# Zeros in place of the identity for TensorE's filling products, and transposes ahead of the modulation products, in an adaLN, sliding-window attention and gMLP kernel on one core

## The chip, the cores and the metric

One core of a Trainium2 chip runs the whole program in one launch. The metric is device time in microseconds (us), the median of several executions. Five engines work from queues of their own and meet at semaphores: TensorE (PE, matrix products; PEld is its weight load), VectorE (DVE), ScalarE (ACT), GpSimd (POOL) and SyncE (SP, which here issues nearly all DMAs).

## The reference, cut to what matters

One sequence of 2048 tokens, width D = 448, 16 heads of 28, window 256, and a gated MLP that mixes over tokens. Only the first stage bears on the change: the modulation rows, the first layer norm, and q, k, v of the first 512 tokens.

```python
mod = (_silu(c) @ w_mod).reshape(c.shape[0], 6, 1, -1)
sa, ca, ga, sb, cb, gb = (mod[:, i] for i in range(6))
h = _layernorm(x, axis=-1) * (1 + ca) + sa
x = x + ga * _A_ref(h, A_wqkv, A_wo)        # q, k, v; 16 heads; window 256; softmax
h = _layernorm(x, axis=-1) * (1 + cb) + sb
x = x + gb * _B_ref(h, B_w_in, B_w_sp, B_b_sp, B_w_out)   # gelu, layernorm, token mix
```

## The kernel before, in words

The 2048 tokens are 16 tiles of 128, in four blocks of 512. All operations are collected as numbered `Op`s with their dependences; the order in which each engine gets them is written out by hand in the table `ORDER` (line 19). A word such as `57.p.0` is operation 57 on PE with buffer 0 of its pool (p PE, a ACT, v DVE, g POOL, s SP). `Sched.order` (line 149) reads the table, and `Sched.waits` derives the semaphore waits. So an operation's number, given by the place in the code where it is added, and its place in the table are all that decides.

The head of the program works like this:

- SP issues loads: x in blocks of four tiles, `w_mod` in four chunks of rows for the first two modulation vectors (`t_wmA`) and the rest later (`t_wmB`, lines 407 and 408), the q, k weights in four chunks (`t_wq`), the v weights.
- DVE sets constants (lines 489 to 496), then computes the layer norm's statistics of tiles 0 to 3 (`stats`, lines 576 to 582, the power on POOL) and the normalised tiles `xn` (`norm`, line 589).
- PE turns the row c into a column (line 518). ACT makes silu of it, `sc_sb` (lines 522 and 523). Four groups of eight products with one column each (line 535), one for each chunk of `w_mod`, make the first two modulation vectors; DVE adds the four up into `modT` (line 540).
- PE transposes the four normalised tiles (line 620, eight at a time here), DVE and ACT scale and shift them with `modT` into `hT`, one chunk of 128 rows at a time (lines 630 and 631). The chunk `WQK` of the weights is copied into a padded layout by ACT, DVE and POOL (lines 568 and 569).
- 32 products of 512 columns (line 640), eight groups of four chunks, make q and k of the first 512 tokens in seven banks of PSUM; ACT and DVE take them out (lines 648 and 649). Then come first scores (line 849), values (line 660), the other modulation vectors as rows (line 553), and the transposes (line 708) of tiles 4 to 7, which POOL and DVE have normalised (lines 593, 595, 589); DVE's line 718 makes `hT` of them, and line 731 their q and k.

Between the real products PE runs filling products (`warm`, line 543): the identity times itself, into bank 5 of PSUM, which nothing reads. They depend on the identity (`t_ident`), which POOL makes at the start. 64 are declared, 40 with 512 columns and 24 with 128; those that the table names are issued, 13 of 512 and 12 of 128 columns.

Of the kernel before, what the change touches and what calls it, by code (L numbers as in the profile page):

```python
# [5 lines left out]
BF16 = mybir.dt.bfloat16  # L6
# [13 lines left out]
0.a 26.v 1.s 2.s 3.s 34.g 23.v 24.v 27.v 43.a 4.s 35.g 5.s 36.g 44.p.0 6.s 138.v 40.g 50.a 32.g 7.s 136.v 37.g 139.v 8.s 25.v 137.v 142.v 140.g 38.g  # L20
9.s 144.v 141.g 10.s 145.v 28.v 143.v 45.a 11.s 46.a 146.g 148.v.0 57.p.0 58.p.0 59.p.0 60.p.0 61.p.0 62.p.0 63.p.0 52.p.1 147.g 97.p.0 53.p 150.v.1
12.s 98.p.0 149.p.2.3 151.p 13.s 152.v.2 54.p 154.v.3 14.s 99.p.0 153.p 29.v 155.p 15.s 55.p 16.s 56.v 132.a 156.v 21.s 133.v 157.a 158.v 64.p.0
65.p.0 66.p.0 67.p.0 68.p.0 69.p.0 190.p.4 17.s 100.p.0 170.p.5 134.g 101.p.0 185.p.6 159.v 18.s 102.p.0 160.p.0 135.a 103.p.0 171.p 104.p.0 161.p
105.p.0 191.p 49.g 106.p.0 175.p.1 107.p.0 162.p 47.a 108.p.0 176.p 195.p.2 165.p.3 42.g 192.p 41.g 163.p 212.v 166.p 164.a 172.p 177.p 214.v 167.p
48.a 173.p 51.v 178.p 213.v 216.v 196.p 168.p 174.a 218.v 186.p 197.p 169.a 198.p 39.v 180.p.0 179.a 187.p 217.v 219.v 193.p 215.v 199.v 188.p 220.g
194.a 181.p 221.g 182.p 30.v 183.p 189.a 373.p.0 184.v 204.p.1 374.a.0 228.g 224.g 210.s 226.g 222.g 121.p.0 227.v.0 225.g.1 211.s 200.p.6 223.v.2
19.s 229.g.3 122.v 205.a 379.p.0 124.s 201.v 230.p.0 380.a.1 209.s 233.p.1 231.v 123.s 234.v 398.p.0 232.a 202.p.6 208.s 235.v 399.a.2 268.v 250.p.0
31.v 270.v 400.a 242.p.1 375.v 264.v 125.s 251.a 405.p.0 266.v 126.s 406.a.3 240.p.0 243.v 269.v 265.v 267.v 238.p.1 271.v 203.v 407.a 272.g 273.g
241.v 376.p.0 239.a 401.v 425.p.0 377.v 236.p.0 278.g 426.a.4.0 381.v 276.g 318.v 33.g 427.p.0 280.g 279.v.0 378.p 262.p.1 274.g 319.v 281.v.1 284.s
275.g.2 320.v 237.a 433.p.0 383.v 277.g.3 246.p.0 263.v 434.a.5.1 282.s 408.v 382.p 128.g 248.p.1 247.v 283.s 321.v 410.v 384.p 428.a 454.p.0 130.g  # L30
249.v 244.p.0 455.a.6.2 385.v 322.v 285.s 131.g 386.v.0 206.p.1 324.v 402.p.0 255.s 456.p.0 245.v 207.a 462.p.0 457.a 252.s 403.v 258.p.1 463.a.0.3
437.v 254.s 438.v 404.p 409.p 387.s 260.p.0 429.v 430.v 411.p 261.a 483.p.0 253.s 412.v 286.v 435.p.0 484.a.1.4 413.v.1 256.p.0 458.v 431.p.0 287.v
432.p 289.v 439.p 257.v 436.a 491.p.0 288.v 259.a 464.p.0 488.v 440.p 492.a.2.0 294.p.0 325.v 459.v 441.v 304.p.1 487.v 465.a 323.v 442.v.2 326.g
512.p.0 295.a 327.g 467.v 443.s 514.p.0 513.a.3.1 460.p.0 466.v 461.p 290.p.0 334.g 496.v 414.s 129.g 305.v 468.p 515.a 520.p.0 291.v 328.g 469.p
521.a.4.2 330.g 335.v.0 296.p.1 332.g 331.v.1 329.g.2 470.v 471.v.0 485.p.0 444.p.0 495.v 472.s 486.a 541.p.0 297.a 445.v 493.p.0 542.a.5.3 489.p.0
446.v 22.s 388.p.1 333.v.3 336.s 525.v 490.p 302.p.0 389.v 494.a 516.v 337.s 549.p.0 303.a 524.v 300.p.1 550.a.6.4 545.v 338.s 390.v 292.p.0 517.v
497.p 301.a 339.s 553.v 551.p.0 498.p 293.a 570.p.0 499.v 552.a 500.v.2 473.p.1 309.s 571.a.0.0 306.s 298.p.0 474.v 308.s 475.v 522.p.0 518.p.0 501.s
523.a 554.v 519.p 299.a 578.p.0 447.v 546.v 316.p.1 579.a.1.1 340.g 307.s 476.v 526.p 575.v 527.p 310.p.0 477.g 341.v 478.g 391.v 317.a 528.v 343.v
572.p.0 529.v.1 479.g 599.p.0 573.a 342.g 311.v 415.p.1 530.s 600.a.2.2 448.g 583.v 543.p.0 502.p.0 449.g 416.v 20.s 392.g 574.v 547.p.0 544.a 607.p.0
503.v 548.p 417.v 555.p 608.a.3.3 504.v 314.p.1 418.v 419.g 556.p 450.g 393.g 348.p.0 557.v 604.v 315.a 420.g 580.p.0 582.v 628.p.0 581.a 558.v.0  # L40
344.p.1 629.a.4.4 505.v 603.v 559.s 576.p.0 506.g 345.v 394.g 577.p 451.g.0 601.p.0 584.p 349.a 507.g 632.v 636.p.0 602.a 585.p 508.g 395.v.1
637.a.5.0 350.p.1 480.g.2 452.v 421.g 586.v 453.s 611.v 609.p.0 346.p.0 587.v.2 351.a 641.v 657.p.0 610.a 588.s 605.p.0 347.v 658.a.6.1 560.p.1 612.v
127.s 659.p.0 396.v 640.v 606.p 397.s 613.p 422.g.0 561.v 660.a 665.p.0 481.v 614.p 661.v 666.a.0.2 312.p.0 354.s 633.v 482.s 630.p.0 562.v 531.p.1
615.v 563.v 313.a 616.v.1 564.g 686.p.0 509.g.1 631.a 532.v 356.p.0 687.a.1.3 423.g 662.v 424.s 634.p.0 670.v 635.p 638.p.0 357.v 642.p 355.s 639.a
533.v 694.p.0 617.s 643.p 691.v 695.a.2.4 688.p.0 360.p.1 534.v 644.v 690.v 353.s 535.g 669.v 589.p.0 352.s 361.a 565.g 645.v.0 715.p.0 689.a 510.g
590.v 646.s 566.g 364.p.1 838.g 716.a.3.0 699.v 663.p.0 667.p.0 511.s 365.v 664.p 671.p 668.a 591.v 723.p.0 720.v 672.p 724.a.4.1 618.p.0 698.v 592.v
696.p.0 593.g 619.v 370.p.1 840.g 863.s 673.v 697.a 674.v.2 567.g.2 744.p.0 371.v 358.p.0 745.a.5.2 536.g 675.s 620.v 537.g 692.p.0 594.g 719.v 693.p
700.p 595.g 855.s 538.v.0 717.p.0 359.a 596.g.1 752.p.0 718.a 728.v 701.p 753.a.6.3 647.p.1 539.g 702.v 540.s 703.v.1 746.p.0 362.p.0 648.v 621.v
749.v 747.a 773.p.0 704.s 622.g 748.v 721.p.0 774.a.0.4 676.p.1 623.g 727.v 624.g 725.p.0 597.v 677.v 722.p 598.s 729.p 756.v 726.a 781.p.0 363.a
568.v 757.v 754.p.0 569.s 730.p 755.a 841.v 368.p.1 731.v 782.a.1.0 732.v.0 366.p.0 369.v 733.s 750.p.0 778.v 775.p.0 785.v 802.p.0 776.a 751.p 777.v  # L50
803.a.2.1 758.p 759.p 783.p.0 760.v 705.p.1 761.v.2 367.a 810.p.0 762.s 706.v 784.a 779.p.0 806.v 811.a.3.2 780.p 812.p.0 786.v 734.p.0 372.s 678.v
787.p 679.v 788.p 707.v 813.a 680.g 763.p.1 839.g 649.v 843.a 789.v 804.p.0 681.g 814.v 887.p.0 870.s 805.a 708.v 807.v 842.a 888.p.1 709.g 790.v.1
710.g 844.a 866.s 889.p 815.v 845.a 625.g.0 735.v 808.p.0 809.p 764.v 711.g 816.p 817.p 650.v 890.p 791.s 818.v 891.a 834.g 819.v.0 923.p.3 736.v
837.g 924.p.2 820.s 765.v 766.v 626.g 925.p 898.a 651.g 652.g 926.p 627.s 653.g 905.p.0 712.g.1 934.a 1031.p.1 682.g 713.v 893.v 767.g 927.a 836.g
714.s 906.p.2 654.v.2 907.p 655.v 935.v 656.s 792.p.0 683.v.0 909.a 684.g 832.g 821.p.1 793.v 685.s 900.v 908.p 768.g 822.v 941.p.0 769.g 916.a 910.v
# [211 lines left out]
def bass_adaLN_cond__sliding_block__mixer_gmlp__prompt_kernel(  # L267
# [42 lines left out]
    x_sb, _, _ = alloc("x_sb", [128, NT, D], BF16)  # L310
# [144 lines left out]
    def dve(dur, fn, deps=(), prio=0.0, take=()):  # L455
        return add({"dve": (dur, fn)}, deps, prio, take)
# [731 lines left out]
```

## Time and profile before

| | |
|---|---|
| median of three runs | 281.51 us (278.8, 281.51, 282.39) |
| the profiled execution | 280.97 us, span of its instructions 279.2 us |
| busy PE, DVE, ACT, POOL | 268.2, 164.0, 128.5, 110.6 us |
| filling products (line 546) up to 30 us | 25, 8.2 us busy |
| first q, k products (line 640) | 32, 7.6 us in all up to 19.4 us |

How to read it: the page's times are of one execution; its span runs from the first to the last instruction, and 1.8 us of the execution's time lie around it. The chain of waits is followed back from the last instruction to what released each step. The timeline lists instructions in order of time, with the start in us, the length of a row of equal instructions, the engine (SPq is SP's issue of a DMA), the line of the code, and in brackets the idle time ahead of it and what ended it. A matmul's length contains its way through the array, so back-to-back products are timed by their starts.

### The profile page before, as it was taken

Reading aid. Unit: us, or ns where it says so; the run is one execution under the profiler, and the core shown is the slowest. Engines: PE = TensorE matmul, PEld = TensorE weight load, DVE = VectorE, ACT = ScalarE, POOL = GpSimd, SP = SyncE. Lnnn points to the kernel's source line nnn. Section 1 sums busy time; section 2 is a strip of 40 time slices with the busy share of each in tenths; the row PEclk is TensorE's granted clock in tenths of the full one; section 3 lists DMA queues with packets and bytes.
Section 4 is the critical chain, followed back from the end, with each engine's and each line's share of the span. In section 5 each row is a group of like instructions: output and inputs, shape, how many; then the busy total and the mean of one; then the engine's idle time right before and its main releaser. Section 6 shows DMA issues by size and latency. Waiting matters only on the chain.

```text
span 279.2 us, 7360 instructions
## 1 busy us (share of the span) xinstructions
PE 268.2 (96%) x3204; PEld 140.8 (50%) x3204; DVE 164.0 (59%) x364; ACT 128.5 (46%) x152; POOL 110.6 (40%) x185
## 2 busy tenths in 40 slices
PE   5999999998999996999999999999999999999995
PEld 2644556565577574544444444444444444454452
DVE  7478999997899899578599501100240300242543
ACT  3579999997999997856767500000000000000000
POOL 4441824216634623676349401321271640271400
PEclk9999999999999999999999999999999999999999
DMA  6997472465744676949799999100000000001113
GB/s 191 302 263 159 103 88 32 90 85 137 158 69 70 95 105 70 215 76 187 86 166 207 170 181 196 20 0 0 0 4 0 0 0 2 0 0 33 57 63 112
DMA packets 66862, 26.48 MB, mean 95 GB/s; under 512 B 57801, under 2 KB 65742, under 8 KB 66830
## 3 DMA queue, kind: packets, MB, share of 16 engines
q1 hardware_dynamic: 66828, 26.01, 48.1%
q8 instruction: 25, 0.41, 0.7%
q14 instruction: 7, 0.06, 0.1%
q10 hardware_dynamic: 2, 0.00, 0.0%
HBM read 9.47 MB, written 1.84 MB: 41 GB/s over the span
## 4 chain that ended last, share of the span: by engine, by line
PE 80%; DVE 9%; POOL 4%; DMA 3%; ACT 2%; issue 1%
PE ps L1073 35%; PE ps L1090 7%; PE ps L1028 7%; PE ps L918 5%; PE ps L731 4%; PE ps L875 4%; PE ps L1049 4%; PE ps L943 3%; POOL rs_all L582 3%; DMA hT<-o_sb 3%; DVE st_all L576 3%; PE ps L773 2%; PE ps L640 2%; DVE PT L891 2%; PE ps L884 2%; PE ps L760 1%
## 5 line engine op out<-in xcount | busy, mean ns | idle before, releaser
L836 ACT ACTIVATE PW<-ps 128x2048 bf16<-128x2048 f32 (+1 forms) x56 | 67.2, 1243 | 7.2 <-PE ps L884 2.3
L1077 DVE TENSOR_TENSOR tmpg<-ps,bsp_bc 128x512 bf16<-128x512 f32 x28 | 19.0, 690 | 74.5 <-PE ps L1073 64.4
L1080 POOL TENSOR_TENSOR z1T<-tmpg,z1T 128x512 bf16<-128x512 bf16 x28 | 31.7, 1151 | 73.5 <-DVE tmpg L1077 73.5
L1073 PE MATMUL ps<-wspB,z 128*128 128x512 bf16 x224 | 49.5, 379 | 0.0
L1073 PE MATMUL ps<-wspA,z 128*128 128x512 bf16 x224 | 49.2, 379 | 0.1
L891 DVE TENSOR_TENSOR PT<-PW,mask 128x1024 bf16<-128x1024 bf16 x56 | 36.7, 681 | 0.3 <-ACT PW L836 0.3
L1073 PEld LDWEIGHTS ps<-wspA,z 128*128 128x128 bf16 x224 | 21.8, 98 | 26.8 <-DVE z L1040 0.6
L1073 PEld LDWEIGHTS ps<-wspB,z 128*128 128x128 bf16 x224 | 21.9, 98 | 26.3
L581 POOL TENSOR_SCALAR ve_all<-mv_all 128x1 f32<-128x1 f32 (+2 forms) x37 | 10.7, 296 | 48.2 <-DVE mv_all L579 47.6
L582 POOL TENSOR_TENSOR rs_all<-ve_all,neghalf 128x1 f32<-128x1 f32 (+2 forms) x37 | 25.5, 698 | 1.0
L918 PE MATMUL ps<-Vaug,PT 128*128 128x29 bf16 x496 | 24.9, 176 | 0.0
L918 PEld LDWEIGHTS ps<-Vaug,PT 128*128 128x128 bf16 x496 | 22.3, 96 | 4.4 <-DVE o_sb L934 1.0
L1028 PE MATMUL ps<-w_in,hT 64*128 64x448 bf16 x224 | 22.9, 349 | 0.0
L1049 PE MATMUL ps<-hT,w_in 64*128 64x512 bf16 x196 | 22.5, 376 | 0.0
L918 PE MATMUL ps<-Vaug,PW 128*128 128x29 bf16 x224 | 20.4, 175 | 0.6 <-issue 0.6
L1090 PE MATMUL ps<-w_out_g,z1T 128*128 128x448 bf16 x105 | 20.7, 352 | 0.0
L731 PE MATMUL ps<-hT,WQK 128*128 128x512 bf16 x80 | 20.1, 380 | 0.2 <-DVE qT L737 0.2
L576 DVE BATCH_NORM_STATS2 st_all<-x_sb 128x6 f32<-128x448 bf16 x32 | 19.0, 614 | 2.2 <-DMA x_sb<-in_A_x_dram 2.1
L576 DVE BATCH_NORM_STATS2 st_all<-z 128x6 f32<-128x448 bf16 x32 | 18.5, 605 | 2.1 <-ACT z L1035 1.9
L918 PEld LDWEIGHTS ps<-Vaug,PW 128*128 128x128 bf16 x224 | 17.7, 96 | 2.9 <-issue 0.7
L1057 ACT ACTIVATE z1T<-ps 128x512 bf16<-128x512 f32 x28 | 14.8, 610 | 7.1 <-PE ps L1049 7.0
L943 PE MATMUL ps<-wo_g,hT 128*128 128x448 bf16 x64 | 14.6, 353 | 3.4 <-DMA hT<-o_sb 3.4
(111 smaller groups left out, 330.8 us busy)
## 6 DMA issues: line engine op xcount, KB each, us to landing
out_dram<-fin SPq DMA_DIRECT2D x15, 112.0 KB, 1.7
x_sb<-in_A_x_dram SPq DMA_DIRECT2D x3, 448.0 KB, 6.8
w_in<-in_B_w_in_dram SPq DMA_DIRECT2D x1, 1344.0 KB, 7.4
wmod<-in_w_mod_dram SPq DMA_DIRECT2D x1, 1296.0 KB, 10.8
QBD<-qT SPq DMA_DIRECT2D x16, 64.0 KB, 3.0
w_out_g<-in_B_w_out_dram SPq DMA_DIRECT2D x1, 784.0 KB, 6.3
wmod<-in_w_mod_dram SPq DMA_DIRECT2D x3, 240.0 KB, 4.7
wq_st<-in_A_wqkv_dram SPq DMA_DIRECT2D x3, 224.0 KB, 5.5
```

Of the source, the lines that this page charges most:

```text
L576: st = [dve(0.62 if True else 0, lambda e, t=t, ci=ci, s=s: e.bn_stats(st_all[:, slot, t, ci, :], s()), deps(t), prio) for ci, s in enumer ...
L582: rs = pool(0.53 + 0.15 * len(tiles), lambda e: e.tensor_tensor(rs_all[:, slot, a:b], ve_all[:, slot, a:b], neghalf[:, 0:b - a], ALU.pow), ...
L731: m = pe(4 * MMS, [lambda e, h=h, g=g, kc=kc, tb=tb: e.matmul(ps[:, h.slot[0], :], lhsT=WQK[:, kc, 4 * g:4 * g + 4, :].rearrange("p a b -> ...
L836: ex = act(xdur, lambda e, out_ap=out_ap, in_ap=in_ap: e.activation(out_ap(), in_ap(), ACT.Exp, scale=SCALE), [s], v - 8.0 + u, takes, tab ...
L891: return dve(0.70, lambda e: e.tensor_tensor(cols(hp.slot[0] * 2048 + 1024 * k, [[256, 4], [128, 2], [1, 128]]), cols(at_w() + 128 + 192 * ...
L918: fns.append(lambda e, hp=hp, hO=hO, hi=hi, bi=bi, kb=kb, hd=hd, nb=nb, a=at[hi][bi], p_of=p_of: e.matmul(ps[:, hO.slot[0], 32 * hd:32 * h ...
L943: mo = pe(4 * MMD, [lambda e, h=h, j=j, ch=ch: e.matmul(ps[:, h.slot[0], 0:D], lhsT=hT[:, ch, j * 128:(j + 1) * 128], rhs=wo_g[:, ch, :], ...
L1028: return lambda e, kc, p0, start, stop: e.matmul(ps[:, hs[t % 2].slot[hf], 0:D], lhsT=hT[p0:p0 + 64, kc, t * 128:(t + 1) * 128], rhs=w_in[ ...
L1049: return lambda e, kc, p0, start, stop: e.matmul(ps[:, hs[b // 2].slot[b % 2], :], lhsT=w_in[p0:p0 + 64, kc, ft * 128:(ft + 1) * 128], rhs ...
L1073: m = pe(16 * MMS, [lambda e, h=h, si=si, ft=ft, tb=tb: e.matmul(ps[:, h.slot[0], :], lhsT=z2[:, si, ft * 128:(ft + 1) * 128], rhs=(wspA i ...
L1080: u = pool(1.16, lambda e, ht=ht, ft=ft, tb=tb: e.tensor_tensor(z1T[tb][:, ft, :], tmpg[:, ht.slot[0], :], z1T[tb][:, ft, :], ALU.mult), [ ...
L1090: return [lambda e, ft=ft: e.matmul(ps[:, h.slot[0], 0:D], lhsT=z1T[t // 4][:, ft, (t % 4) * 128:(t % 4 + 1) * 128], rhs=w_out_g[:, ft, :] ...
```

## The change

A tile `wz` of 128 x 128 bf16 is added and set to zero by DVE, as the first operation of the table. The filling products multiply `wz` by itself and wait for that memset instead of for the identity. 17 filling products are issued, all of 512 columns; the twelve of 128 columns are gone, nine of which stood among the q, k products. The new operation moves every later number up by one, so all words of the table read otherwise; the order on ACT, POOL and SP is the same, DVE's has the memset in front, and PE's differs up to the end of the q, k products.

```diff
+    wz, _, _ = alloc("wz", [128, 128], BF16)
...
+    t_wz = dve(0.08, lambda e: e.memset(wz[:], 0.0), prio=-99.9)
+
     def warm(n, dur, times, cols):
         for _ in range(n):
             hW = Hold(bH)
             hW.until.append(pe(dur, [lambda e, hW=hW: e.matmul(
-                ps[:, hW.slot[0], 0:128 * cols].rearrange("p (a b) -> p a b", b=128), lhsT=ident[:], rhs=ident[:].unsqueeze(1).broadcast_to([128, cols, 128]),
-                start=True, stop=True) for _ in range(times)], [t_ident], 900.0, [hW]))
+                ps[:, hW.slot[0], 0:128 * cols].rearrange("p (a b) -> p a b", b=128), lhsT=wz[:], rhs=wz[:].unsqueeze(1).broadcast_to([128, cols, 128]),
+                start=True, stop=True) for _ in range(times)], [t_wz], 900.0, [hW]))
```

The first words of the table, before and now:

```diff
-0.a 26.v 1.s 2.s 3.s 34.g 23.v 24.v 27.v 43.a 4.s 35.g 5.s 36.g 44.p.0 6.s
+57.v 0.a 26.v 1.s 2.s 3.s 34.g 23.v 24.v 27.v 43.a 4.s 35.g 5.s 36.g 58.p.0 59.p.0 60.p.0 44.p.0 6.s
```

PE's queue from its start to the end of the modulation, before. `ident` lines are fillers, `one,c_row` is the column of c, `sc_sb,wmod` the modulation groups, `ident,xn` the transposes:

```order
L518 MATMUL ps<-one,c_row 128x1 x3
L518 MATMUL ps<-one,c_row 64x1
L546 MATMUL ps<-ident 128x512 x7
L535 MATMUL ps<-sc_sb,wmod 128x1 x8
L546 MATMUL ps<-ident 128x128
L535 MATMUL ps<-sc_sb,wmod 128x1 x8
L546 MATMUL ps<-ident 128x128
L620 MATMUL ps<-ident,xn 128x128 x8
L535 MATMUL ps<-sc_sb,wmod 128x1 x8
L546 MATMUL ps<-ident 128x128
L620 MATMUL ps<-ident,xn 128x128 x8
L535 MATMUL ps<-sc_sb,wmod 128x1 x8
```

The same stretch now (line numbers are up by one to three; `wz` lines are fillers):

```order
L549 MATMUL ps<-wz 128x512 x3
L519 MATMUL ps<-one,c_row 128x1 x3
L519 MATMUL ps<-one,c_row 64x1
L549 MATMUL ps<-wz 128x512 x10
L623 MATMUL ps<-ident,xn 128x128 x8
L536 MATMUL ps<-sc_sb,wmod 128x1 x16
L549 MATMUL ps<-wz 128x512
L536 MATMUL ps<-sc_sb,wmod 128x1 x8
L623 MATMUL ps<-ident,xn 128x128 x8
L536 MATMUL ps<-sc_sb,wmod 128x1 x8
```

Three fillers stand ahead of the column of c and ten behind it, the first eight transposes come before the first two modulation groups, and one filler of 512 columns is left between the groups in place of three of 128.

PE's queue from the end of the modulation to the modulation rows (line 553), before; a product and a small filler alternate nine times:

```order
L546 MATMUL ps<-ident 128x512 x6
L640 MATMUL ps<-hT,WQK 128x512
L546 MATMUL ps<-ident 128x128
...
L640 MATMUL ps<-hT,WQK 128x512 x23
L849 MATMUL ps<-qT,KT 128x128 x8
L660 MATMUL ps<-wv,hT 128x448 x4
L553 MATMUL ps<-wmod,sc_rep 32x448 x16
```

and now:

```order
L549 MATMUL ps<-wz 128x512 x3
L643 MATMUL ps<-hT,WQK 128x512 x32
L852 MATMUL ps<-qT,KT 128x128 x8
L663 MATMUL ps<-wv,hT 128x448 x4
L556 MATMUL ps<-wmod,sc_rep 32x448 x16
```

Three fillers stand ahead of the q, k products in place of six, and none among them; what follows is unchanged.

More of the change, by code (lines that the diff above doesn't have):

```diff
@@ L24 @@
[L24 to L31, printed above, removed]
@@ L72 @@
[L72 to L74 removed]
+57.v 0.a 26.v 1.s 2.s 3.s 34.g 23.v 24.v 27.v 43.a 4.s 35.g 5.s 36.g 58.p.0 59.p.0 60.p.0 44.p.0 6.s 139.v 40.g 50.a 32.g 7.s 137.v 37.g 140.v 8.s
@@ new lines @@
+474.p.1 310.s 572.a.0.0 307.s 299.p.0 475.v 309.s 476.v 523.p.0 519.p.0 502.s 524.a 555.v 520.p 300.a 579.p.0 448.v 547.v 317.p.1 580.a.1.1 341.g
+308.s 477.v 527.p 576.v 528.p 311.p.0 478.g 342.v 479.g 392.v 318.a 529.v 344.v 573.p.0 530.v.1 480.g 600.p.0 574.a 343.g 312.v 416.p.1 531.s
+601.a.2.2 449.g 584.v 544.p.0 503.p.0 450.g 417.v 20.s 393.g 575.v 548.p.0 545.a 608.p.0 504.v 549.p 418.v 556.p 609.a.3.3 505.v 315.p.1 419.v 420.g
+557.p 451.g 394.g 349.p.0 558.v 605.v 316.a 421.g 581.p.0 583.v 629.p.0 582.a 559.v.0 345.p.1 630.a.4.4 506.v 604.v 560.s 577.p.0 507.g 346.v 395.g
@@ new lines @@
+578.p 452.g.0 602.p.0 585.p 350.a 508.g 633.v 637.p.0 603.a 586.p 509.g 396.v.1 638.a.5.0 351.p.1 481.g.2 453.v 422.g 587.v 454.s 612.v 610.p.0
+347.p.0 588.v.2 352.a 642.v 658.p.0 611.a 589.s 606.p.0 348.v 659.a.6.1 561.p.1 613.v 128.s 660.p.0 397.v 641.v 607.p 398.s 614.p 423.g.0 562.v 661.a
+666.p.0 482.v 615.p 662.v 667.a.0.2 313.p.0 355.s 634.v 483.s 631.p.0 563.v 532.p.1 616.v 564.v 314.a 617.v.1 565.g 687.p.0 510.g.1 632.a 533.v
+357.p.0 688.a.1.3 424.g 663.v 425.s 635.p.0 671.v 636.p 639.p.0 358.v 643.p 356.s 640.a 534.v 695.p.0 618.s 644.p 692.v 696.a.2.4 689.p.0 361.p.1
@@ new lines @@
+535.v 645.v 691.v 354.s 536.g 670.v 590.p.0 353.s 362.a 566.g 646.v.0 716.p.0 690.a 511.g 591.v 647.s 567.g 365.p.1 839.g 717.a.3.0 700.v 664.p.0
+668.p.0 512.s 366.v 665.p 672.p 669.a 592.v 724.p.0 721.v 673.p 725.a.4.1 619.p.0 699.v 593.v 697.p.0 594.g 620.v 371.p.1 841.g 864.s 674.v 698.a
+675.v.2 568.g.2 745.p.0 372.v 359.p.0 746.a.5.2 537.g 676.s 621.v 538.g 693.p.0 595.g 720.v 694.p 701.p 596.g 856.s 539.v.0 718.p.0 360.a 597.g.1
+753.p.0 719.a 729.v 702.p 754.a.6.3 648.p.1 540.g 703.v 541.s 704.v.1 747.p.0 363.p.0 649.v 622.v 750.v 748.a 774.p.0 705.s 623.g 749.v 722.p.0
@@ L75 @@
+1215.p.1 1188.v.3 1185.v.0 1216.p 1211.p.3 1186.s 1217.v.1 1218.s 1212.p 1189.s 1223.p.7 1213.v.2 1214.s 1220.p 1224.p 1178.p.6 1221.v.0 1225.v.1
+1222.s 1226.s 1179.v.3 1180.s
 """
```

87 lines of the change are left out of this document (40 added, 47 removed).

## The prediction, as put on record

> **What bounds the kernel now.** I read the page first, then the chain of waits in order of time over the first 35 us, then the timeline of that stretch engine by engine, then the DMA issues. The change touches only work before the first attention scores, so the question is what sets the end of that head, and who takes over from it.
>
> From the page, the span, the granted clock in 40 slices and the chain's shares by engine:
>
> ```profile
> span 279.2 us, 7360 instructions
> PEclk9999999999999999999999999999999999999999
> PE 80%; DVE 9%; POOL 4%; DMA 3%; ACT 2%; issue 1%
> ```
>
> The chain runs through PE for 80% of the span; whatever moves PE's queue as a whole is seen at the end. The chain's own rows in the head (start, length, engine, tile, line):
>
> ```profile
> 1.13 1.18 DVE wmod L491
> 9.81 2.16 PE ps L546 x6
> 14.41 4.96 PE ps L640 x23
> 20.46 0.87 PE ps L553 x16
> 21.33 0.86 PE ps L660 x4
> 22.20 0.22 PE ps L849 x8
> 22.42 0.57 PE ps L708 x8
> 23.01 1.00 DVE hT L718 x2
> ```
>
> So DVE's memsets and statistics open the chain, six filling products (L546) hold it for 2.16 us, the first q, k products (L640) until 19.4, then modulation rows and values, and at 22.4 the transposes (L708) of the next four tiles. What the fillers cost and at which speed TensorE ran is in its timeline:
>
> ```profile
> 2.60 0.35 PE L518 MATMUL ps<-one,c_row 1*128 1x1 bf16 x4 [2.60 <-DVE one L490]
> 2.89 3.17 PE L546 MATMUL ps<-ident 128*128 128x512 bf16 x7
> 7.38 1.06 PE L620 MATMUL ps<-ident,xn 128*128 128x128 bf16 x8
> 9.41 0.40 PE L535 MATMUL ps<-sc_sb,wmod 128*128 128x1 bf16 x8
> 9.67 2.30 PE L546 MATMUL ps<-ident 128*128 128x512 bf16 x6
> 11.80 0.38 PE L640 MATMUL ps<-hT,WQK 128*128 128x512 bf16 x1
> 12.08 0.38 PE L640 MATMUL ps<-hT,WQK 128*128 128x512 bf16 x1
> 14.25 5.13 PE L640 MATMUL ps<-hT,WQK 128*128 128x512 bf16 x23
> ```
>
> The seven fillers from 2.89 take 3.17 us; less the last one's latency that is 0.43 us for a 512-column product. The 23 products from 14.25 take 5.13 us, 0.216 us each. TensorE thus ran at half pace in the first stage although the page's row of granted clock prints a 9 everywhere. Five of the six fillers from 9.67 still ran at 0.43 (9.67 plus five times 0.426 is 11.80), so the pace doubled at about 11.4. Inside the q, k stage a product and the small filler behind it take 12.08 - 11.80 = 0.27 us, so a filler of 128 columns costs 0.055 us at full pace.
>
> By the Trainium skill, page TensorE: Matmul & The Clock Gate, section "What's actually happening", the clock gate opens after a sufficiently busy window of about 3.4 us of a free-running clock; the trace agrees that the pace is binary (0.43 against 0.216) and cannot show the window.
>
> **The change, part by part.** *The zeros.* A memset of 128 x 64 words is put first on DVE. Rows of memsets, two of which size it and the third of which is the last step before the modulation's input:
>
> ```profile
> 8.59 0.43 DVE L494 MEMSET wq_st<- 64x448 uint32 x1
> 18.70 0.24 DVE L495 MEMSET wv<- 64x224 uint32 x1
> 6.22 0.06 DVE L493 MEMSET sc_sb<- 1x1 bf16 x1
> ```
>
> Halving the columns takes off 0.19, which leaves 0.05 fixed and 0.06 for 64 columns: 0.11 us, and everything behind it on DVE starts that much later, since L491 and the statistics form the chain. PE pays 0.11 where it waits for the normalised tiles.
>
> *Fillers from 1.4 us.* The zeros are there at 1.24, so three fillers run from about 1.4 to 2.68 at 0.43. The products of c, queued behind them, start at 2.68 and not 2.60; nobody feels it, since DVE's own sc_sb step at 6.2 ends last for what follows. Then ten more: 4.3 us at the slow pace, to 7.25 at latest. The fillers cost nothing as long as they end before the normalised tiles come. Before, 3 us of fillers were followed by work of one column and transposes, and the pace doubled late. Now some 5.5 us of fillers stand almost without a gap. I take it that the pace doubles inside this run: 1.7 us of fillers sufficed from 9.67, with transposes ahead of them. The other bound is that it does not double until the q, k products, which is a rival below.
>
> *Transposes before the modulation.* The times of their inputs, and of what hangs on the modulation:
>
> ```profile
> 6.42 0.70 DVE L589 TENSOR_SCALAR xn<-x_sb,mv_all,rs_all 128x448 bf16<-128x448 bf16 x2
> 7.74 0.70 DVE L589 TENSOR_SCALAR xn<-x_sb,mv_all,rs_all 128x448 bf16<-128x448 bf16 x2 [0.61 <-POOL rs_all L582]
> 3.26 0.59 SPq L417 DMA_DIRECT2D wmod<-in_w_mod_dram  x1
> wmod<-in_w_mod_dram SPq DMA_DIRECT2D x1, 120.0 KB, 5.4
> 9.84 0.19 DVE L540 TENSOR_REDUCE modT<-ps 128x8 f32<-128x32 f32 x1 [0.82 <-PE ps L535]
> 10.07 0.54 DVE L631 TENSOR_SCALAR hT<-ps,modT 128x512 bf16<-128x512 bf16 x1
> 10.65 0.78 ACT L630 ACTIVATE hT<-ps,modT 128x512 bf16<-128x512 bf16 x1 [0.65 <-DVE hT L631]
> 10.99 0.93 POOL L569 COPY WQK<-wq_st 128x896 bf16<-128x896 bf16 x1 [3.29 <-DMA wq_st<-in_A_wqkv_dram]
> 11.53 0.95 ACT L568 ACTIVATE WQK<-wq_st 128x896 bf16<-128x896 bf16 x1
> ```
>
> Tile 1 is normalised at 7.12 + 0.11 = 7.23, so PE's transposes of tiles 0 and 1 end at about 7.5 (0.055 each at full pace, instead of 1.06 for eight, 0.85 of it without the tail). Two modulation groups of 0.26 (9.67 - 9.41) reach 8.0, a filler 8.2, the third group 8.5, the transposes of tiles 2 and 3 (input at 8.44 + 0.11) 8.95, the fourth group 9.2 and its result 9.35. Its weights were issued at 3.26 and need 5.4: they land at 8.66, in time. So modT's reduction starts at 9.35 in place of 9.84, and hT's first chunk (0.23 later, 0.54 long) is there at 10.12. The three fillers after the last group end at 9.85, ahead of it. q, k start at 10.15 and not 11.80: 1.65 us earlier. This term stands between -0.1 us (slow pace throughout: 7.25 + 0.85 + 0.52 + 0.43 + 0.26 + 0.85 + 0.4 = 10.56 for modT, three slow fillers from 10.4 to 11.7) and 1.65; I take 1.65, as the pace should have doubled.
>
> *No fillers inside q, k.* Nine of 0.055 go: 0.5 us. Their cover would be a wait for WQK. Its third chunk is ready at 10.99 + 0.93 = 11.92, set by a load; the ninth product needs it, and would be due at 10.15 + 8 x 0.216 = 11.88, so it waits under 0.1. The fourth chunk (11.53 + 0.95 = 12.48) is needed by the fourteenth product, due at 13.0: no wait.
>
> Sum to the end of q, k: 1.65 + 0.5 - 0.05 = 2.1 us earlier, 17.3 in place of 19.4.
>
> *What is late next.* The 2.1 us do not reach the next stage whole:
>
> ```profile
> 14.00 1.15 DVE L576 BATCH_NORM_STATS2 st_all<-x_sb 128x6 f32<-128x448 bf16 x2 [2.05 <-DMA x_sb<-in_A_x_dram]
> 17.71 0.23 POOL L581 TENSOR_SCALAR ve_all<-mv_all 128x4 f32<-128x4 f32 x1 [4.39 <-DVE mv_all L579]
> 19.18 0.96 POOL L593 TENSOR_SCALAR ve_all<-mv_all,rs_all 128x1 f32<-128x1 f32 x4
> 20.12 1.52 POOL L595 TENSOR_SCALAR xn<-x_sb,rs_all,ve_all 128x448 bf16<-128x448 bf16 x2
> 22.35 1.07 PE L708 MATMUL ps<-ident,xn 128*128 128x128 bf16 x16
> 7.78 0.51 SPq L407 DMA_DIRECT2D wmod<-in_w_mod_dram  x1
> 8.33 0.50 SPq L408 DMA_DIRECT2D wmod<-in_w_mod_dram  x1
> wmod<-in_w_mod_dram SPq DMA_DIRECT2D x1, 1296.0 KB, 10.8
> wmod<-in_w_mod_dram SPq DMA_DIRECT2D x1, 216.0 KB, 11.2
> ```
>
> Tiles 4 to 7 of x land at 14.00 and go through DVE's statistics, POOL's variance, scale and normalising without PE: the last two normalised tiles are ready at 20.12 + 1.52 = 21.64. L708 stood at 22.35 and can start no earlier than 21.68. The modulation rows (L553) wait for weights that land at 7.78 + 10.8 = 18.6 and 8.33 + 11.2 = 19.5, so PE, 2.1 us early, waits before them for about 1 us. From 19.55 the rows, values and scores take 0.87 + 0.86 + 0.22 and end at 21.5, still before 21.68. Both limits are loads whose issues the change leaves alone. So of 2.1 us, 22.35 - 21.68 = 0.67 us pass on; DVE's hT (23.01) and all behind it follow PE by it. Behind it the chain is made of durations and of transfers issued by the work itself, so nothing fixed in time remains to catch it. What would: a queue that fills differently later; bounds 0 and 2.1.
>
> Sum against the profiled execution: 280.97 - 0.67 = 280.3 us. That execution lies 0.54 below the median shown, 281.51, and inside its runs, 278.8 to 282.39; I predict 280.3 for the median as well, since the changed kernel depends less on when the pace doubles.
>
> **The rivals.** *All of it arrives.* If the x tiles land earlier than in this execution or L708 is reached by less than I think, 2.1 us carry: 278.9. For it: slack of the DVE chain at 14.00 is just a DMA's landing, which may vary. Against it: two separate loads say otherwise.
>
> *Nothing arrives.* ACT's exponentials and DVE's masks run side by side with PE after 30 us; if one of them has its own pace there, 0.67 us vanish: 281.0. For it: the gain is small against the spread of 3.6 us of the runs. Against it: the chain's rows are 80% PE.
>
> *The gate is shut when q, k begin.* Zeros might not count as activity, or the stage of transposes and one-column products might close it again. Place: the 32 q, k products. They start at 11.7 by the slow sum above, no fillers stand among them, and each slow one costs 0.21 more. The slow spell lasts between 1.7 us (9.67 to 11.4) and 8.5 us (2.89 to 11.4), so 4 to 20 products, 0.85 to 4.2 us. They end at 11.7 + 6.9 + 0.85 to 4.2, that is 19.45 to 22.8 against 19.2 on the same count: 0.25 to 3.6 later, middle 1.9, and PE's queue carries this whole: 282.9. It decides as soon as more than four products run at 0.43. Against it: real fillers did open it with transposes between them.
>
> The Trainium skill, page TensorE: Matmul & The Clock Gate, Part 4, says that transposes do not count as busy for the gate, which speaks for a gate that closes in this stage; and its section "What's actually happening" says the monitor watches how busy PE was, which speaks against zeros being ignored. No row here separates the two.
>
> **How the numbers follow.** Forecast 280.3: 0.47. Nothing arrives, 281.0: 0.25. All arrives, 278.9: 0.12. Gate shut, 282.9: 0.12. Others 0.04. The range reaches from below the second-best case, with half a spread of the runs, to the gate's middle: 278.0 to 282.8. 2% of 281.5 is 5.6 us, about what a measurement of this kernel can tell from no change; no case reaches it. I leave 0.03 on each side for what I have not seen: faster 0.03, within 0.94, slower 0.03.
>
> **What would show it.** Right: fillers going from 0.43 to 0.216 us before 7.3; modT's reduction near 9.35; the first q, k product near 10.15 and 32 of them in 6.9 to 7.0 us; PE idle about 1 us before the rows product, named as waiting for a DMA of wmod; L708's successor at 21.7. Wrong: q, k products of 0.43; modT after 9.84; no wait at the rows; or the transposes of tiles 4 to 7 earlier than 21.

## The result and the profile after

The changed kernel takes 278.09 us in the median of 21 executions (276.39 to 280.85); beside it the kernel before took 280.01 us in the median of 21 (278.16 to 282.55). The ratio is 0.9946, 95% interval 0.9921 to 0.9971: faster by about half a per cent, some 1.5 us, and far from 2%. The ratios leave out executions more than 1.5% above the fastest of their kernel, and the spans of two profiles (of the first and the eighth experiment), in which TensorE's clock was halved for stretches of 3.41 us, are not used.

The page of the changed kernel has the span, the clock, the chain by engine and the queue that brings code:

```profile
span 276.3 us, 7323 instructions
PEclk9999999999999999999999999999999999999999
q8 instruction: 25, 0.41, 0.6%
PE 79%; DVE 6%; DMA 5%; ACT 4%; SPq 2%; POOL 1%; issue 1%
```

The span is 2.9 us shorter than in the profile before. DMA has 5% of the chain where it had 3%, DVE 6% for 9%. The chain of the changed kernel's head shows why:

```profile
7.14 6.91 DMA x_sb<-in_A_x_dram
14.07 1.15 DVE st_all L579 x2
...
17.25 0.45 DVE mv_all L582 x2
18.09 1.06 POOL rs_all L585
19.24 0.96 POOL ve_all L596 x4
20.21 1.64 POOL xn L598 x2
21.98 0.62 PE ps L711 x8
22.62 1.01 DVE hT L721 x2
```

No PE row stands ahead of 21.98 any more: the load of x tiles 4 to 7, their statistics and POOL's normalising set the end of the head. Before, PE's fillers and q, k products stood there. The timeline of the same execution, rows of PE, DVE and ACT:

```profile
1.04 1.46 PE L549 MATMUL ps<-wz 128*128 128x512 bf16 x3 [1.04 <-DVE wz L544]
3.08 4.43 PE L549 MATMUL ps<-wz 128*128 128x512 bf16 x10
...
7.32 0.63 PE L623 MATMUL ps<-ident,xn 128*128 128x128 bf16 x8
...
9.26 0.81 PE L549 MATMUL ps<-wz 128*128 128x512 bf16 x3
9.44 0.19 DVE L541 TENSOR_REDUCE modT<-ps 128x8 f32<-128x32 f32 x1 [0.21 <-PE ps L536]
9.48 0.95 ACT L571 ACTIVATE WQK<-wq_st 128x896 bf16<-128x896 bf16 x1 [2.75 <-DMA wq_st<-in_A_wqkv_dram]
9.66 0.54 DVE L634 TENSOR_SCALAR hT<-ps,modT 128x512 bf16<-128x512 bf16 x1
10.23 0.40 DVE L572 COPY WQK<-wq_st 128x896 bf16<-128x896 bf16 x1
...
10.54 1.42 PEld L643 LDWEIGHTS ps<-hT,WQK 128*128 128x128 bf16 x8 [0.97 <-DVE hT L634]
...
10.79 6.85 PE L643 MATMUL ps<-hT,WQK 128*128 128x512 bf16 x31 [0.72 <-DVE WQK L572]
...
19.65 0.53 PEld L556 LDWEIGHTS ps<-wmod,sc_rep 128*32 128x32 bf16 x16 [0.61 <-DVE qT L652]
...
21.98 1.05 PE L711 MATMUL ps<-ident,xn 128*128 128x128 bf16 x16 [0.27 <-POOL xn L598]
```

Ten fillers take 4.43 us, so they are slow (0.43 us each) nearly to their end; eight transposes behind them take 0.63 us where they took 1.06. The row of the q, k products has 31 of the 32, and the missing record is the first: its weight load (PEld) stands at 10.54, and 32 products, which take 7.07 us in runs 1 and 10 below, end at 10.79 + 6.85 = 17.64 if they begin at 10.57 (before 11.80). The wait that the row names is therefore not that of the first product. The products run without a gap at full pace, and the transposes of tiles 4 to 7 begin at 21.98 (before 22.35). The head has gained 0.37 us.

Where the other 2.5 us of this pair of profiles came from is read off by pairing instructions. The pair lies 2.9 us apart, more than the 1.5 us of the many executions, so part of what follows is the spread between executions. ACT issues the same 152 instructions in both kernels, so each has a twin; the start of five of them, in us:

| ACT instruction | before | after | gain so far |
|---|---|---|---|
| number 24 | 26.23 | 25.84 | 0.39 |
| number 59 | 62.31 | 62.49 | -0.18 |
| number 74 | 79.64 | 78.28 | 1.36 |
| number 104 | 112.77 | 110.00 | 2.77 |
| the last | 159.92 | 157.14 | 2.78 |

The head's 0.39 us stand for every ACT instruction from 23.6 to 50.9 us and are gone at 51.4. The gain arises in two later stretches, 62 to 80 us and 105 to 113 us, which the change does not touch. The chains of waits name what stands there. In the kernel before:

```profile
62.17 3.50 DMA hT<-o_sb
...
73.45 0.62 issue
...
107.02 4.03 DMA hT<-o_sb
```

and in the changed one:

```profile
60.97 4.05 DMA hT<-o_sb
...
103.09 3.83 DMA hT<-o_sb
```

SyncE transposes the attention's output `o_sb` by DMA into `hT`, and PE's products of the output projection (line 943, now 946) wait for it. PE's waits between 20 and 115 us (total, times, longest, in us), before:

```profile
PE ps L943 <- DMA hT<-o_sb: 3.4, 3, 1.3
PE ps L918 <- issue: 0.6, 1, 0.6
```

and after:

```profile
PE ps L946 <- DMA hT<-o_sb: 1.6, 3, 0.8
PE ps L734 <- issue: 0.3, 2, 0.2
```

The wait for these transposes shrank by 1.8 us, the one for nothing that the profile shows by 0.3; new short waits for DVE's `hT` and `PT`, 0.5 us in all, take some of it back. All the waits in this view from the transposes of tiles 4 to 7 on come to 4.2 us before and 2.6 after; with the head's 0.37 that is 2.0 of the 2.9 us, and the rest is not accounted for. SyncE's own timeline shows why the transposes were late, in the kernel before:

```profile
54.87 5.33 SPq L479 DMA_TRANSPOSE hT<-xn  x3
60.24 1.89 SPq L674 DMA_DIRECT2D QBD<-qT  x3
62.17 2.28 SPq L479 DMA_TRANSPOSE hT<-o_sb  x1
```

and in the changed one:

```profile
55.76 2.59 SPq L480 DMA_TRANSPOSE hT<-xn  x2
58.40 2.53 SPq L677 DMA_DIRECT2D QBD<-qT  x3
60.97 1.27 SPq L480 DMA_TRANSPOSE hT<-o_sb  x1
```

SyncE issues in order. Three transposes take 5.33 us before, because the third of them, from 57.50, took 2.70 in place of 1.27; the transpose of `o_sb` behind them starts at 62.17 and not 60.97, and takes 2.28 itself. In the trace of before, fetches of pieces of PE's code began at 57.4 and 62.2, where these two issues begin; after, at 58.3, where a plain DMA's issue begins, and at 62.9. The plain DMA was not spared: the three issues for `QBD` took 2.53 us in place of 1.89, but the transpose of `o_sb` behind them took 1.27. A piece is 16 KB, 25 for the program (the row of the instruction queue above), one for every 128 weight loads with their products. In 14 profiles, between 28 and 112 us, 137 transposes had such a fetch start between 0.1 us ahead of their issue and 1.2 us behind it: their median is 1.98 us, and 63% of them took over 1.7. The 332 others have a median of 1.27, and 9% over 1.7. Plain issues for `QBD` in the same stretch go the same way: 1.48 us in the median for the 23 with such a start up to 0.55 us behind, 0.60 for the 145 others. This is a count over the profiles; no run moved a fetch and nothing else.

The Trainium skill, page Runtime: NRT & Kernel Launch, section "Instruction fetch mechanics", has code arrive in blocks of 16 KiB, 256 instructions, at a cost that is mostly hidden. The size agrees with this trace; for SyncE's issues beside a fetch the cost is not hidden, by the medians above.

### The profile page after: what moved, and what is told of

Its sections match the earlier page's. It is cut to its first block, busy times and chain, and to the rows that moved or that the text cites. A ratio compares the mean times of both kernels' runs of the same rounds, so it can differ in the third digit from the quotient of the medians.

```text
span 276.3 us, 7323 instructions
## 1 busy us (share of the span) xinstructions
PE 265.9 (96%) x3174; PEld 139.4 (50%) x3196; DVE 163.8 (59%) x365; ACT 128.3 (46%) x152; POOL 110.0 (40%) x185
## 4 chain that ended last, share of the span: by engine, by line
PE 79%; DVE 6%; DMA 5%; ACT 4%; SPq 2%; POOL 1%; issue 1%
PE ps L1076 35%; PE ps L1031 8%; PE ps L1052 8%; PE ps L1093 7%; PE ps L921 5%; PE ps L734 4%; PE ps L878 4%; PE ps L946 3%; ACT PW L839 3%; DMA hT<-o_sb 3%; PE ps L776 3%; DMA x_sb<-in_A_x_dram 3%; DVE st_all L579 2%; PE ps L887 2%; PE ps L763 1%
## 5 line engine op out<-in xcount | busy, mean ns | idle before, releaser
L921 PE MATMUL ps<-Vaug,PT 128*128 128x29 bf16 x496 | 24.8, 176 | 0.0
L921 PEld LDWEIGHTS ps<-Vaug,PT 128*128 128x128 bf16 x496 | 22.3, 96 | 4.4 <-DVE o_sb L937 1.0
L921 PE MATMUL ps<-Vaug,PW 128*128 128x29 bf16 x224 | 20.4, 175 | 0.0
L734 PE MATMUL ps<-hT,WQK 128*128 128x512 bf16 x69 | 17.9, 380 | 1.4 <-issue 0.3
L921 PEld LDWEIGHTS ps<-Vaug,PW 128*128 128x128 bf16 x224 | 17.7, 96 | 2.2
L1038 ACT ACTIVATE z<-ps 128x896 bf16<-128x896 f32 x16 | 14.1, 914 | 7.1 <-PE ps L1031 7.1
```

Source lines behind the costliest of these rows:

```text
L734: m = pe(4 * MMS, [lambda e, h=h, g=g, kc=kc, tb=tb: e.matmul(ps[:, h.slot[0], :], lhsT=WQK[:, kc, 4 * g:4 * g + 4, :].rearrange("p a b -> ...
L921: fns.append(lambda e, hp=hp, hO=hO, hi=hi, bi=bi, kb=kb, hd=hd, nb=nb, a=at[hi][bi], p_of=p_of: e.matmul(ps[:, hO.slot[0], 32 * hd:32 * h ...
```

## The experiments

Two explanations had to be told apart. *The head*: the earlier q, k products, or the fillers taken out from among them, carry to the end. *The position of the code*: the number of PE instructions issued in the head decides where every later fetch falls beside SyncE's transposes, and the change happened to move it to a better place. Of three batches each ran on one chip with 34 or 35 executions of the kernel before. Ratios are against those, with 95% intervals.

**1. Order without zeros.** The new table, but fillers that multiply the identity:

```diff
-                ... lhsT=wz[:], rhs=wz[:].unsqueeze(1)...  [t_wz], 900.0, [hW]))
+                ... lhsT=ident[:], rhs=ident[:].unsqueeze(1)...  [t_ident], 900.0, [hW]))
```

> The changed order of PE's queue, but the fillers multiply the identity again, which POOL has ready at about 1.7 us (the zeros were there at 1.0). Theory: order and number of the fillers do it, the operand only sets their first start. 13 fillers from 1.8 us, the pace of TensorE doubles before the transposes or soon behind them, first q, k product at 10.5 to 10.9 us, transposes of tiles 4 to 7 at 21.9 to 22.1, ratio to before 0.993 to 0.998. Rival (the zeros' 0.7 us matter): the pace doubles a window later than in the changed kernel, 3.4 us, some q, k products run at 0.43 us, ratio 0.998 to 1.003.

277.38 us, ratio 0.9929 (0.9899 to 0.9959). First filler at 1.77 us, q, k at 10.83, transposes of tiles 4 to 7 at 22.09. The new table alone, that is the order and number of the fillers, brings all of it; the zeros have no part that can be measured.

**2. Zeros without the order.** The old order of PE's work, with its 25 fillers, and the memset in front:

```diff
-57.v 0.a ... 36.g 58.p.0 59.p.0 60.p.0 44.p.0 ... 149.v.0 148.g
+57.v 0.a ... 36.g 44.p.0 ... 149.v.0 58.p.0 59.p.0 60.p.0 61.p.0 62.p.0 63.p.0 64.p.0 52.p.1 148.g 98.p.0
```

> The order of before, with the zeros as operand of all 25 fillers, and the memset first on DVE. Theory: the operand alone moves nothing, since the first filler still stands behind the column of c; DVE starts 0.1 to 0.2 us later; first q, k product at 11 to 12 us, ratio to before 0.999 to 1.002. Rival (zeros do not count as activity): the pace doubles later than 11.4 us, q, k products of 0.43 us, ratio 1.002 to 1.012.

278.73 us, ratio 1.0022 (0.9989 to 1.0055): the zeros alone bring nothing. The q, k products begin at 12.24, a little later than expected, and run at full pace. With as many fillers as the kernel before, its profile has only 0.7 us of waits for `o_sb`, where that kernel's has 3.4.

**3. The new order without any filler.**

```diff
-... 36.g 58.p.0 59.p.0 60.p.0 44.p.0 ... 12.s 61.p.0 ... 70.p.0 150.p.2.3 ... 53.p 71.p.0 54.p ... 159.v 72.p.0 73.p.0 74.p.0 191.p.4
+... 36.g 44.p.0 ... 12.s 150.p.2.3 ... 53.p 54.p ... 159.v 191.p.4
```

> The changed kernel without any of its 17 fillers; the memset stays. Theory: the pace has not doubled when the q, k products begin at about 10.6 us; 4 to 16 of them run at 0.43 us instead of 0.216, 0.85 to 3.4 us more, so they end at 18.5 to 21 us (17.5 with fillers); the first 1.5 us of that are free, since the load of x holds the next stage, the rest is paid: transposes of tiles 4 to 7 at 22.0 to 23.8, ratio to before 0.996 to 1.006. Rival (the fillers do nothing, the order alone brings the gain): products at 0.216 us, ratio as the changed kernel, 0.992 to 0.997.

277.66 us, ratio 0.9943 (0.9915 to 0.9971), as good as the change. Its timeline of PE (q, k products; the transposes of tiles 4 to 7):

```profile
10.91 9.21 PE L642 MATMUL ps<-hT,WQK 128*128 128x512 bf16 x32 [0.88 <-DVE hT L633]
...
23.10 1.07 PE L710 MATMUL ps<-ident,xn 128*128 128x128 bf16 x16
```

The 32 products take 9.21 us in place of 7.07, since the pace doubles only at 15.3, and the transposes begin at 23.10, 0.75 us later than in the kernel before. Yet the span is 275.8 us. PE's waits:

```profile
PE ps L945 <- DMA hT<-o_sb: 0.3, 1, 0.3
```

The wait for `o_sb` is all but gone. A head that ends later went with a total that is shorter: the head theory fails here.

**4. One more cap taken off the head.** DVE's memset of `Vaug` (operation 39) is recorded with 0.27 us, but the aggregations beside it start 0.77 us late, so it was put ahead of the statistics:

```diff
-... 164.p 213.v 167.p ... 199.p 39.v 181.p.0
+... 164.p 39.v 213.v 167.p ... 199.p 181.p.0
```

> The changed kernel, with DVE's memset of Vaug's ones moved from behind the statistics of tiles 4 to 7 into DVE's wait ahead of them. Theory (the chain from the load of tiles 4 to 7 sets the end of the head): the three aggregations start at 16.5 and not 17.25 us, the transposes of tiles 4 to 7 at 21.2 to 21.4 instead of 22.0, and the whole is 0.6 to 0.8 us shorter than the changed kernel: ratio to before 0.990 to 0.994. Rival (the middle of the kernel, with its own transposes by DMA, sets the pace and takes such gains in): as the changed kernel, 0.9946.

277.27 us, ratio 0.9935 (0.991 to 0.996), within the change's own interval. Its timeline of DVE and PE:

```profile
16.36 0.37 DVE L582 BATCH_NORM_AGGREGATE mv_all<-st_all 128x2 f32<-128x6 f32 x3
...
19.89 0.94 PE L556 MATMUL ps<-wmod,sc_rep 128*32 128x448 bf16 x16 [1.06 <-DVE xn L592]
...
21.85 1.07 PE L711 MATMUL ps<-ident,xn 128*128 128x128 bf16 x16
```

The aggregations come 0.89 us earlier (17.25 to 16.36), but the transposes only 0.13. PE now stands 1.06 us ahead of the modulation rows; the engine named had finished at about 19.75, 0.14 us earlier, and the products also need the last chunks of `w_mod`. The last of these is what ended last: issued at 8.39, it needs 11.4 us and lands at 19.80, and PE's first weight load for the rows starts at 19.86. The expected 21.2 to 21.4 was not reached.

**5. The change with 25 fillers**, as many as before; two of 512 columns give way to ten of 128, in the same place:

```diff
-61.p.0 ... 68.p.0 69.p.0 70.p.0 150.p.2.3
+61.p.0 ... 68.p.0 98.p.0 99.p.0 ... 107.p.0 150.p.2.3
```

> The changed kernel with eight fillers more, so that PE has as many instructions ahead of the q, k products as the kernel before (25 fillers): in the run of ten, two of 512 columns are replaced by ten of 128 columns, which takes as long. Position theory (PE's code arrives in pieces of 16 KB; where in the queue a piece ends decides which products wait for code in the middle of the kernel, whatever the first 22 us do): the wait of an L918 product for 'issue' at 73 us is back, 0.3 to 0.6 us, and most of the gain is gone, ratio to before 0.998 to 1.002. Head theory (the head's 0.4 us and the steadier pace give the gain): as the changed kernel, 0.992 to 0.997.

278.58 us, ratio 0.9987 (0.9953 to 1.002). The head is as good as the change's or better (q, k at 10.37, by the first weight load at 10.34; transposes at 21.77), and the gain is not seen, though the interval still touches the change's. PE's wait for `o_sb` is 2.6 us. The other sign that the position theory named, a wait of an L918 product (now L921) for `issue` at 73 us, is not back.

**6. The kernel before with 17 fillers.** Eight of the small ones among the q, k products taken out:

```diff
-170.p.5 134.g 101.p.0 185.p.6 159.v 18.s 102.p.0 160.p.0 135.a 103.p.0 171.p 104.p.0 161.p
+170.p.5 134.g 185.p.6 159.v 18.s 160.p.0 135.a 171.p 161.p
```

> The kernel before without eight of the nine fillers of 128 columns among the q, k products, 17 fillers in all as in the changed kernel; order and operand as before. Position theory: PE's code then stands where the changed kernel has it; no wait for 'issue' at 73 us, ratio to before 0.993 to 0.997. Head theory: the q, k products end 0.44 us earlier, of which 0 to 0.4 arrives: ratio 0.998 to 1.001.

278.21 us, ratio 0.9993 (0.9961 to 1.0025). By the position it should have had the change's gain, and it has not. Its pace doubled only at 14.1 us and the transposes began at 23.63. This run speaks against the position alone.

**7. The kernel before without fillers** (all 25 words taken out).

> The kernel before without any of its 25 fillers, order otherwise as before (modulation ahead of the transposes). Position theory: PE's code stands as in the changed kernel without fillers, 25 products less; ratio 0.993 to 0.997 although the q, k products run at 0.43 us and the transposes of tiles 4 to 7 come 0.7 to 2 us later than in the kernel before. Head theory: ratio 1.002 to 1.008.

277.7 us, ratio 0.9961 (0.9929 to 0.9994): faster, with q, k products that take 9.85 us (9.46 for the 31 recorded; the first lacks its record) and transposes at 23.94, 1.6 us later than with fillers. PE never waits for `o_sb` in its profile. In this kernel the fillers bought nothing at all.

**8. The kernel before again**, as a measure of what a batch can tell.

> The kernel before once more, unchanged. Both theories: ratio 0.997 to 1.003. Position theory: its profile again has the L918 wait for 'issue' of 0.3 to 0.6 us at 73 us, at the same product. Head theory: the wait is chance and may be absent; the pace doubles at another time than 11.4 us, and the transposes of tiles 4 to 7 move with it, by up to 1 us.

279.49 us, ratio 1.0016 (0.9979 to 1.0054), as both theories have it. The wait for `issue` at 73 us is absent here too, with the same program: the position theory's sign fails, and that wait does not go with the position.

**9 to 12, on one chip.** All four have the change's order: nine with eight small fillers behind the q, k products, where PE is idle (25 in all), ten the change itself, eleven with 81 fillers (half a piece of code more), twelve with 145 (a whole piece more). The edits are

```diff
-... 190.a 374.p.0
+... 190.a 98.p.0 99.p.0 100.p.0 101.p.0 102.p.0 103.p.0 104.p.0 105.p.0 374.p.0
```

for nine; and for eleven (groups of 16, 16, 16, 16 and 5 in place of five fillers) and twelve (eight groups of 16 and one of 9 in place of nine fillers)

```diff
+    def tiny(times):
+        hW = Hold(bH)
+        hW.until.append(pe(0.03 * times, [lambda e, hW=hW: e.matmul(
+            ps[:, hW.slot[0], 0:8], lhsT=wz[:], rhs=wz[:, 0:8], start=True, stop=True) for _ in range(times)], [t_wz], 900.0, [hW]))
```

> The changed kernel with eight small filling products of 128 columns put back, 25 in all, but behind the q, k products, in TensorE's idle time before the modulation values, so that the head stays as it is. Theory A (the number of TensorE instructions ahead sets where the fetches of its code fall beside SyncE's transposes later on): as the run with 25 fillers in the changed order, ratio 0.998 to 1.002 against the kernel before, and pieces of code fetched at the times of that run less the head's shift. Theory B (the gain is the earlier head or the smaller number of fillers inside the q, k products): ratio 0.992 to 0.997 as for the change itself. Q, k products from 10.8 us and the transposes of tiles 4 to 7 near 22.0 under both.

> The changed kernel unchanged, on the same chip as the three others, as their measure: ratio 0.992 to 0.997 under every theory. A ratio over 0.998 would say that differences of half a per cent between batches are not the kernel's.

> Five of the ten 512-column fillers replaced by 69 products of 8 columns: 81 fillers in place of 17, 64 pairs of weight load and product more, half a piece of TensorE's code. Theory A (position of the code): every later piece is fetched half a piece of work earlier, so the ratio may be anything from 0.99 to 1.005, and is outside 0.992 to 0.997 if the position of the change was a lucky one; the long issues of SyncE's transposes move to other transposes. Theory B (head): 0.992 to 0.997, as the run without fillers shows that a late gate costs nothing.

> Nine of the ten 512-column fillers replaced by 137 products of 8 columns: 145 fillers, 128 pairs more than the change, one whole piece of code. Theory A (position of the code): the pieces fall where they fall in the changed kernel, so ratio 0.992 to 0.997. Theory B (head): 0.992 to 0.997 too, if the gate opens late, since the run without fillers had that ratio. A ratio over 0.999 speaks against both.

| | fillers | q, k from | tiles 4 to 7 from | median | ratio |
|---|---|---|---|---|---|
| nine | 25 | 10.69 | 22.26 | 278.64 | 0.9993 (0.995 to 1.0037) |
| ten | 17 | 10.30 | 21.80 | 277.61 | 0.9972 (0.9938 to 1.0006) |
| eleven | 81 | 11.23 | 22.95 | 278.97 | 1.0008 (0.997 to 1.0047) |
| twelve | 145 | 11.40 | 22.54 | 277.8 | 0.9961 (0.9928 to 0.9994) |

Nine, ten and twelve came out where the position put them, the repetition at the edge of its interval; for eleven the position allowed nearly any ratio, so that run speaks against the head alone. One by one the intervals overlap. Taken in pairs, the means of ten and twelve (277.90, 277.69) lie 1.04 us under those of nine and eleven (278.59, 279.08), 95% interval 0.4 to 1.7 from the spread of their executions. Part of this is the half-pace stretches described below, which 4 of the 12 executions of eleven have: without such executions it is 0.66 us, 0.1 to 1.2. Twelve has 128 weight loads and products more than the change and a head that ends 0.56 us later, and keeps its gain. Its page and its waits:

```profile
q8 instruction: 26, 0.43, 0.7%
```

```profile
PE ps L946 <- DMA hT<-o_sb: 0.7, 1, 0.7
```

One piece of code more was fetched, and between 50 and 105 us the fetches begin within 0.6 us of those in the changed kernel, but for one (89.5 for 88.3). The repetition shows the limit of this. Its SyncE, in the same stretch as above, and its waits:

```profile
54.80 5.29 SPq L480 DMA_TRANSPOSE hT<-xn  x3
60.13 1.89 SPq L677 DMA_DIRECT2D QBD<-qT  x3
62.06 2.25 SPq L480 DMA_TRANSPOSE hT<-o_sb  x1
```

```profile
PE ps L946 <- DMA hT<-o_sb: 3.2, 2, 1.7
```

The same program as the change, and in this execution the long transposes of the kernel before: the fetch came at 57.3, a microsecond earlier than in the first profile. Its span is 278.1 us in place of 276.3. So a position does not fix the collision; executions of one kernel differ by a microsecond in it, and a position can only make it more or less frequent. Over the twelve profiles without a half-pace stretch the span goes with this wait, correlation 0.74, 0.74 us of span for 1 us of wait; a wait of 0 to 0.7 us goes with 275.8 to 276.8, one of 2.6 to 3.4 with 277.4 to 279.2; between them, at 1.0 to 1.6, the spans lie anywhere from 275.6 to 278.3. By the number of fillers these waits do not separate: 0.7 to 3.2 us in the profiles with 17 or 145, 0.7 to 3.4 in those with 25.

**What stays open.** Shown is that the gain is not the head's (runs 3, 5, 7, 9, 12) and not the zeros' (1, 2), that the spans go with PE's waits for the transposes of `o_sb`, and that SyncE's issues take longer where a piece of code is fetched. That the position decides the mean is not shown: run 6 has the change's number and none of its gain, and single profiles of one number differ as much as those of different numbers. In runs 3, 6 and 7 the pace in the head moves too, and with it when everything later meets. A second, smaller difference was counted and not tried: stretches of half pace (a mean granted clock under 0.9965) occurred in 36 of 140 executions with the old order and fillers, and in 7 of 116 of the others, eleven (4 of 12) left aside. They do not make the difference, since it is as large among executions without one (first batch: 279.03 before, 277.11 and 277.24 for runs 1 and 4, in the mean).

## Why the prediction was right or wrong, point by point

**The time.** 280.3 was predicted for the median, 278.09 was measured, at the lower end of 278.0 to 282.8; within 2%, as most of the chance had it. The forecast stood on a median of three executions, 281.51; the 21 beside the change have 280.01, which is already below 280.3. Read as a difference, the sum gave 0.67 us (1.2 from the median shown, of which 0.54 comes from no term of the sum), against about 1.5 us (0.8 to 2.2 from the interval of the ratio). The sign was right, but the mechanism that gave it was not, so that it came out right was luck.

**The zeros.** Said to cost 0.11 us on DVE. The memset's own row is 0.11 us long, as said, but DVE's next memset starts 0.19 us later (1.32 for 1.13), and that of `sc_sb` went from 6.22 to 6.41: 0.08 more than said, and small.

**The pace.** Said to double inside the ten fillers. It doubled at 7.36, at their very end, and between 4.6 and 7.4 in the four other kernels, and the repetition, that have at least eight fillers of 512 columns in that place. In the kernel before four of the six fillers from 9.67 were slow, not five (9.67 + 4 x 0.426 = 11.4, and two of 0.216 end at 11.8); the time that was read, 11.4, is right. The Trainium skill, page TensorE: Matmul & The Clock Gate, section "What's actually happening", makes this a matter of where a free-running window of 3.4 us lies. The first experiment's profile shows such a window:

```profile
86.90:90.30 3.40, 2.16 (x87) 1.80 (x85) 2.51 (x5) 3.18 (x3) 1.48 (x3) 1.00 0.34 72
90.30:93.72 3.42, 3.42 (x16) 1.16 (x17) 1.41 (x3) 0.82 (x2) 2.72 (x7) 0.50 0.47 95
93.72:97.10 3.38, 3.32 (x126) 2.47 (x127) 2.66 (x5) 2.80 (x4) 1.13 (x2) 1.00 0.89 151
```

The columns are the stretch, its length, busy times of PE, PEld, DVE, ACT and POOL, the granted clock, DMA share and GB/s. The clock is 0.50 for 3.42 us, behind a stretch of that length in which PE was busy for 2.16 us. The prediction said that the trace could not show the window; this one does. The other traces agree: full pace lasted 259.41 us in run 3, 266.24 in run 2, 269.65 in the kernels before and after and 273.07 in run 5, which are 76, 78, 79 and 80 times 3.413. Ahead of the doubling PE was busy for the whole of such a window (3.42 us from 7.98 to 11.40 before, 3.41 from 3.95 to 7.36 after), while in run 3 a window with 2.44 us (8.46 to 11.88) did not double the pace. So 1.7 us of fillers had not sufficed in the kernel before: the other half of its window was transposes, products of one column and a small filler.

**The modulation and the first q, k product.** `modT` was due at 9.35 and came at 9.44; the q, k products were due at 10.15 and came at 10.57; they ended at 17.64, where 17.3 was due, 1.7 us earlier than before in place of 2.1. The step that failed is "no wait" for WQK: it went through the third and fourth chunks of the weights, and the first one binds. ACT's copy of it, which waits for a load, ends at 9.48 + 0.95 = 10.43, after the first chunk of `hT` (9.66 + 0.54 = 10.20), and the first weight load follows at 10.54. In run 10 the load landed earlier, the copy ended at 10.16, and the products began at 10.30.

**The cap.** The statement that two loads hold the next stage was right, with the places named: PE's weight loads stand idle for 0.61 us ahead of the modulation rows, until the last chunk of `w_mod` lands (issued at 8.32, 11.3 us to landing, the weight load at 19.65), and the transposes wait for POOL's `xn`. They came at 21.98 for 21.68, POOL's last step ending at 21.83 in place of 21.64. The passing gain was 0.37 us, not 0.67.

**"Everything behind follows".** This is the step that failed: "Behind it the chain is made of durations and of transfers issued by the work itself, so nothing fixed in time remains to catch it." The transfers issued by the work itself are what catches it. At 62 us nothing of the head's gain was left in this pair of profiles, and runs 3, 7 and 12 end 0.2 to 1.6 us later in the head than the kernel before and earlier in total. The bound of "a queue that fills differently later", put at 0 and 2.1 us, was the term that decided, and it was taken at its lower end without a row for it; the profile before had one, 3.4 us of PE waiting for `hT<-o_sb`.

**The rivals.** "Nothing arrives" was the truth about the head, for another reason than DVE's or ACT's pace. "All of it arrives" gave 278.9, the nearest number, by the wrong way. "The gate is shut" did not happen: zeros count as work, since the pace doubled at 7.36 behind a window (from 3.95) filled by products of zeros up to its last 0.04 us. That transposes do not count as busy, the rule that the prediction names for this rival, is not borne out by the kernel before, whose window ahead of 11.40 was half transposes and products of one column. Run 3 has its price, 2.14 us more for the 32 products, and shows that PE's queue does not carry it to the end: that rival's time was as wrong as the forecast's way.

## What to carry to other kernels

Before a gain at the start is carried to the end, list the waits behind it that end on a DMA, and treat their total as the range of what can come of any shift: here 3.4 us of waits for transposes against 0.4 us of shift. When a change in the head moves the total, pair the instructions of one engine in the two traces and look where the gain grows; if it grows where nothing was changed, the same kernel profiled again and kernels that leave the head alone come before any explanation. Fillers that keep the clock up are worth trying without: here neither order lost anything by dropping all of them.

## What the runs showed of the hardware

- A DMA transpose's issue on SyncE beside a fetch of PE's code took 1.98 us in the median, and 1.27 otherwise; a plain issue for `QBD` 1.48 and 0.60. SyncE issues in order, so one such issue delays all behind it (`o_sb` at 62.17 for 60.97 in the first pair of profiles).
- The granted clock fell to half for single stretches of 3.41 us, each behind a stretch of that length in which PE was busy for 2.2 to 2.4 us (90.3 to 93.7 us in run 1; 9.1 to 12.5 and 91.0 to 94.4 in run 8).
- With a memset of 128 x 256, recorded with 0.27 us, in the queue ahead of them, DVE's aggregations came after a gap of 0.77 us; with the memset moved away (run 4) they ran without that gap.
